# Moving operands of the large matmuls stored as even and odd columns in two halves, in an mLSTM kernel with two gated layers on one core

## The chip, the core and the metric

The kernel runs on one core of a Trainium2 chip. The engines named below are TensorE (matmul; its weight loads are listed apart as PEld), VectorE (DVE), ScalarE (ACT), GpSimd (POOL) and SyncE (SP, which issues most transfers). The metric is the device time of one launch in microseconds; lower is better.

## The reference: what is computed

An mLSTM recurrence over 768 steps for 2 batches and 8 heads of 40 features, and then two gated layers over its 1536 tokens of 320 features:

```python
m_new = np.maximum(f_gate[:, :, t] + m, i_gate[:, :, t])
...
C = f_stab[:, :, None, None] * C + i_stab[:, :, None, None] * np.einsum('bhd,bhe->bhde', vt, kt)
n = f_stab[:, :, None] * n + i_stab[:, :, None] * kt
h_tilde = np.einsum('bhde,bhe->bhd', C, qt)
nq = np.einsum('bhd,bhd->bh', n, qt)[:, :, None]
denom = np.maximum(np.abs(nq), 1.0)
...
y[:, :, t] = o * h_tilde / denom
...
gate = 1.0 / (1.0 + np.exp(-(x @ w_gate)))
val = x @ w_val
return (gate * val @ w_out).astype(np.float32)
...
a = x @ w_a
b = x @ w_b
return (a * b @ w_out).astype(np.float32)
```

## The kernel before

The recurrence is done in 12 chunks of 64 steps (`E`, `S`, `st`, `o` matmuls, small ones). Each chunk gives one token tile of 128 tokens (two batches of 64 steps). A token tile is transposed on TensorE (`transp`, line 482, three 128x128 transposes into PSUM), and the transposed tile is split into a high part, rounded to the chip's fp32r type by ScalarE (`x_hi`, line 486), and a low part, the rest, by VectorE (`x_lo`, line 489). Both go into a block `xb`, which holds `[128 partitions, 2 (high, low), 3 feature chunks, 512 tokens]` of 4 bytes each. Four token tiles fill a block; six blocks serve the two layers.

A unit of a layer takes one 128-wide slice `f` of d_ff and two or four token tiles. `mm1` (line 519) makes the gate (`pa`) and the value (`pb`) in eight matmuls each: the weights are the stationary operand, and a row of `xb` (256 or 512 tokens of one feature chunk) is the moving operand, the one that streams through the array. ScalarE and VectorE make the product `g`, its high part `gh` and its low part `gl`. `mm2` (lines 526 to 528, into `acc`) then multiplies by the output weights: `gh` or `gl` is stationary, and the 320 columns of the output weights (`wh`, the high part, or `wl`, the low part) are the moving operand. Three matmuls go to each token tile, so a unit of four tiles issues 16 matmuls in `mm1` and 12 in `mm2`.

The weights come as 64-bit floats, are narrowed on three engines into 32 bits and split into high and low parts in a tile `W` of 2 x 832 + 256 columns; columns 512 to 831 of each part are the output weights. The host lays the weights out in this order (`pack`) without arithmetic.

The order of all tasks on all engines is written out by hand in `PLAN`. There are 24 units of two token tiles (in `HEAD`, between the chunks of the recurrence) and 60 units of four. In all that is 960 matmuls of 512 columns and 384 of 256 columns in `mm1`, and 864 of 320 columns in `mm2`.

Of the kernel before, what the change touches and what calls it, by code (L numbers as in the profile page):

```python
# [7 lines left out]
F32 = mybir.dt.float32  # L8
BF16 = mybir.dt.bfloat16
F32R = mybir.dt.float32r  # L10
# [3 lines left out]
AF = mybir.ActivationFunctionType  # L14
ALU = mybir.AluOpType

P = 128
# [4 lines left out]
DM = H * D  # L22
DFF = 1536
NF = DFF // P
BT = 512
NB = B * S // BT
NT = BT // P
# [24 lines left out]
NH = 4 * P + DM  # L52
# [78 lines left out]
def kernel(  # L131
# [11 lines left out]
    nc = tc.nc  # L143
# [9 lines left out]
    a3 = ctx.enter_context(tc.tile_pool(name="a3", bufs=3))  # L153
# [7 lines left out]
    def ps_tile(b, name):  # L161
        t = pspool.tile([P, 512], F32, tag=slot(b), name=name)
        fill(t, idle.pop() if idle else 0)
        return t
# [107 lines left out]
    def gate_parts(i):  # L272
        c0, n = GCH[i]
        s0 = 0 if i else 1

        def part0():
            g, lf, L, ms = gws[i]
            if i == 0:
                nc.vector.memset(ms[:, 0:1], -1e30)
                nc.vector.memset(lf[:, 0:1], 0.0)  # L280
            else:
                nc.vector.tensor_copy(ms[:, 0:1], mlast[0])
            nc.vector.tensor_tensor_scan(ms[:, 1:], g[:, 1], g[:, 0], ms[:, 0:1], op0=ALU.add, op1=ALU.max)
            mlast[0] = ms[:, n : n + 1]
            nc.vector.tensor_tensor(lf[:, s0:], g[:, 1, s0:], ms[:, s0:n], op=ALU.add)

        def part1():
            g, lf, L, ms = gws[i]
            nc.vector.tensor_tensor(lf[:, s0:], lf[:, s0:], ms[:, s0 + 1 :], op=ALU.subtract)
            nc.vector.tensor_tensor(g[32:64, 0], g[32:64, 0], ms[32:64, 1:], op=ALU.subtract)  # L290

        def part2():
            g, lf, L, ms = gws[i]
            nc.vector.tensor_tensor_scan(L, rm[:, 0:n], lf, 0.0, op0=ALU.mult, op1=ALU.add)
            nc.vector.tensor_tensor(L[32:64], g[32:64, 0], L[32:64], op=ALU.subtract)

        def part3():
            g, lf, L, ms = gws[i]
            hi = g[:, 1].bitcast(F32R)
            nc.scalar.activation(hi, L, AF.Copy)  # L300
            nc.scalar.activation(lf, hi.bitcast(F32), AF.Copy, scale=cs[0:64, C_AB + 1 : C_AB + 2])

        def part4():
            g, lf, L, ms = gws[i]
            nc.vector.scalar_tensor_tensor(
                V[:, c0 : c0 + n], L, cs[0:64, C_AB : C_AB + 1], lf, op0=ALU.mult, op1=ALU.subtract
            )

        return part0, part1, part2, part3, part4
# [78 lines left out]
    Sps, Eps, Sts, Tps = {}, {}, {}, {}  # L388
# [93 lines left out]
            nc.tensor.transpose(v[:, c], src[:, c * P : (c + 1) * P], ident)  # L482
        return v

    def x_hi(v, dst, c0):
        nc.scalar.activation(dst[:, 0, :, c0 : c0 + P], v, AF.Copy)

    def x_lo(v, dst, c0):
        nc.vector.tensor_tensor(
            dst[:, 1, :, c0 : c0 + P], v, dst[:, 0, :, c0 : c0 + P].bitcast(F32), op=ALU.subtract  # L490
        )

    xb = {}

    def xblock(k):
        if k not in xb:
            xb[k] = a3.tile([P, 2, 3, BT], F32R, tag="xb", name=f"xb{k}")
        return xb[k]

    def ph_T(s):  # L500
        Tps[s] = transp(ps_tile("e", f"tp{s}"), xtok[s])

    def ph_xh(s):
        x_hi(Tps[s], xblock(s // NT), (s % NT) * P)

    def ph_xl(s):
        x_lo(Tps[s], xblock(s // NT), (s % NT) * P)


    def mm1(f, l, m, dst, x):  # L510
        w = W[l * NF + f]
        a, al, c = m * 2 * P, NH + m * 2 * P, 2 * NH + m * P
        seq = (
            (a, 0, 0), (a, 1, 0), (al, 0, 0),
            (a + P, 0, 1), (a + P, 1, 1), (al + P, 0, 1),
            (c, 0, 2), (c, 1, 2),
        )
        for i, (w0, h, cb) in enumerate(seq):
            nc.tensor.matmul(dst, w[:, w0 : w0 + P], x[:, h, cb], start=(i == 0), stop=(i == 7))  # L519

    def mm2(f, l, gh, gl, accs, st, sp):
        w = W[l * NF + f]
        wh, wl = w[:, 4 * P : NH], w[:, NH + 4 * P : 2 * NH]
        for i, a in enumerate(accs):
            c = slice(i * P, (i + 1) * P)
            nc.tensor.matmul(a, gh[:, c], wh, start=st, stop=False)  # L526
            nc.tensor.matmul(a, gh[:, c], wl, start=False, stop=False)  # L527
            nc.tensor.matmul(a, gl[:, c], wh, start=False, stop=sp)  # L528
# [47 lines left out]
    def unit_a(u):  # L576
        k, f = UNITS[u]
        l, st0, ns, fs = SEGS[k]
        x = xblock(l * NB + st0 // NT)[:, :, :, (st0 % NT) * P : (st0 % NT + ns) * P]
        pa = ps_tile("mm1", f"pa{u}")  # L580
        pb = None
        if ns == 2:
            pa, pb = pa[:, 0:256], pa[:, 256:512]
        UT[u] = {"x": x, "pa": pa, "pb": pb}
        mm1(f, l, 0, pa, x)

    def unit_b(u):
        k, f = UNITS[u]
        l, t = SEGS[k][0], UT[u]
        if t["pb"] is None:  # L590
            t["pb"] = ps_tile("e", f"pb{u}")
        mm1(f, l, 1, t["pb"], t["x"])
# [72 lines left out]
    for u, (k, f) in enumerate(UNITS):  # L665
        l, st0, ns, fs = SEGS[k]
# [31 lines left out]
    for i, (c0, n) in enumerate(GCH):  # L698
        if i:
            task(f"gl{i}", "D", lambda i=i: load_gates(i))  # L700
        a, b, c, c2, c3 = gate_parts(i)
# [5 lines left out]
    for i in range(NPREP // 2, NSTEP // 2):  # L707
        s = 2 * i
# [54 lines left out]
    for u, (k, f) in enumerate(UNITS):  # L763
        l, st0, ns, fs = SEGS[k]
        c = l * NF + f
# [20 lines left out]
        for i in range(ns):  # L786
            s = st0 + i
# [25 lines left out]
    with tc.manual_schedule():  # L813
        pick("mm1", ())
        first = ps_tile("mm1", "first")
        for entry in PLAN.split():
            entry, _, n = entry.partition("*")
            name, _, e = entry.partition(":")
# [19 lines left out]
def _layout(inputs):  # L838
    import numpy as np

    f32 = np.float32
    q, k, v, og = (np.asarray(inputs[n]) for n in ("q", "k", "v", "o_gate"))
    ig, fg = np.asarray(inputs["i_gate"]), np.asarray(inputs["f_gate"])
    dt = q.dtype
    a = {}


    r = np.arange(32)
    rpair = np.concatenate([r // 8, r % 16 // 4])
    rb = np.concatenate([r // 4 % 2, r // 2 % 2])  # L850
    rpar = np.concatenate([r % 2, r // 16])
    rlo = np.concatenate([r // 2 % 2, r % 2])

    def rows(g):
        return g[rb, 2 * rpair + rpar]

    a["gates"] = np.stack([rows(ig), rows(fg)], 1)

    def tr(z):

        z = z.reshape(B, NPAIR, 2, NSTEP, T, D).transpose(2, 5, 3, 1, 0, 4)
        o = np.zeros((P, NSTEP, NPAIR * B * T), dt)
        o[:D], o[64 : 64 + D] = z.reshape(2, D, NSTEP, NPAIR * B * T)
        return o.transpose(1, 0, 2)

    a["kqT"] = np.concatenate([tr(k), tr(q)], 2)

    def tok(z):

        z = z.reshape(B, NPAIR, 2, NSTEP, T, D).transpose(2, 4, 3, 1, 0, 5)[::-1]  # L870
        return z.reshape(P, NSTEP, NPAIR * B, D)

    vo = np.ones((P, NSTEP, NPAIR * B, E1 + D), dt)
    vo[..., :D] = tok(v)
    vo[..., E1:] = tok(k)
    a["kv"] = vo.reshape(P, NSTEP, -1).transpose(1, 0, 2)
    a["ogate"] = og.reshape(B, H, NSTEP, T, D).transpose(0, 3, 2, 1, 4).reshape(P, NSTEP * H * D)

    def bits(w):
        w = np.ascontiguousarray(w)  # L880
        return w.view(np.int64) if w.dtype.itemsize == 8 else w

    def pack(x, y, z):
        x, y = (bits(w).reshape(DM, NF, P).transpose(1, 0, 2) for w in (x, y))
        o = np.empty((NF, P, NW), x.dtype)
        for i, w in enumerate((x[:, 0:P], x[:, P : 2 * P], y[:, 0:P], y[:, P : 2 * P])):
            o[:, :, i * P : (i + 1) * P] = w
        o[:, :, 4 * P : NH] = bits(z).reshape(NF, P, DM)
        o[:, 0:64, NH:] = x[:, 2 * P :]
        o[:, 64:, NH:] = y[:, 2 * P :]  # L890
        return o

    a["w1"] = pack(inputs["moe_w_gate"], inputs["moe_w_val"], inputs["moe_w_out"])
    a["w2"] = pack(inputs["moe2_w_a"], inputs["moe2_w_b"], inputs["moe2_w_out"])


    c = np.zeros((P, C_N), f32)
    c[:, C_ID : C_ID + P] = np.eye(P)
    blk = np.zeros((64, NPAIR, B, T), f32)
    blk[np.arange(64), rpair, rb] = 1.0  # L900
    c[0:64, C_RE : C_RE + 512] = blk.reshape(64, 512)
    tri = np.where(np.arange(T)[None, :] < np.arange(T)[:, None], -(2.0**100), 0.0)
    c[64:, C_RE : C_RE + 512] = np.tile(tri, (1, NPAIR * B))
    half = np.arange(P) // 64
    for par in range(2):
        d = c[:, C_LD + par * P : C_LD + (par + 1) * P]
        d[0:32] = (rpar[:32] == par)[:, None]
        tk = half == 1 - par
        d[32:64, tk] = (rpar[32:] == par)[:, None]
        d[64:, tk] = np.eye(64)  # L910
    c[0:D, C_IP : C_AB] = np.eye(D)
    c[64 : 64 + D, C_IP : C_AB] = np.eye(D)
    lo = rlo == 1
    c[0:64, C_AB] = lo
    c[0:64, C_AB + 1] = np.where(lo, 1.0, -1.0)
    a["cst"] = c
    return a
# [21 lines left out]
```

## Time and profile before

| | |
|---|---|
| median of three runs | 475.13 us (473.99 to 476.45) |
| the profiled execution's own time | 474.68 us |
| its span, first to last instruction | 472.9 us |
| TensorE busy | 463.2 us, 98% of the span |
| VectorE, ScalarE, GpSimd busy | 62%, 51%, 21% |
| granted TensorE clock | 0.998 of full speed over the span |

The span leaves out 1.8 us of the execution's own time, which lie around it. [...]

### The profile page before, as it was taken

What the parts mean: (1) busy time and instruction counts of PE and PEld (TensorE: products, weight loads), DVE (VectorE), ACT (ScalarE), POOL (GpSimd) and SP (SyncE); (2) the same over time, 40 slices, a digit from 0 to 9 for tenths busy, and PEclk for the clock granted to TensorE, in tenths of its full rate; (3) what the DMA queues carried; (4) which work ended last, traced back from release to release, by engine and by line L of the source; (5) the groups of instructions that cost most, each with busy time, mean ns of one, the idle gap of its engine ahead of it and who ended that gap; (6) DMA issues with size and microseconds to landing.
All of it is one profiled execution on the core that took longest, in us unless ns stands there. A gap on an engine that the chain in (4) does not pass through costs nothing.

```text
span 472.9 us, 8680 instructions
## 1 busy us (share of the span) xinstructions
PE 463.2 (98%) x3516; PEld 403.6 (85%) x3516; DVE 295.0 (62%) x505; ACT 241.3 (51%) x454; POOL 101.2 (21%) x110
## 2 busy tenths in 40 slices
PE   9899999999999999999999999999999999999995
PEld 3478899999998989888888898888989888888885
DVE  6989997998655663637675564664655727524243
ACT  4899888678672635333464442645453415322130
POOL 3133326623340014100320311103140003200000
PEclk9999999999999999999999999999999999999999
DMA  7979445333022040300202220024021020001121
GB/s 230 308 254 264 150 133 144 88 119 114 1 83 85 1 168 20 130 18 1 83 1 83 75 94 1 9 86 156 10 83 74 1 84 1 0 1 27 30 55 55
DMA packets 10454, 39.31 MB, mean 83 GB/s; under 512 B 1840, under 2 KB 3760, under 8 KB 10416
## 3 DMA queue, kind: packets, MB, share of 16 engines
q1 hardware_dynamic: 10128, 38.45, 25.7%
q8 instruction: 27, 0.44, 0.4%
q10 hardware_dynamic: 288, 0.33, 0.2%
q14 instruction: 11, 0.09, 0.1%
HBM read 36.71 MB, written 1.97 MB: 82 GB/s over the span
## 4 chain that ended last, share of the span: by engine, by line
PE 88%; DVE 4%; DMA 3%; ACT 2%; issue 1%; SPq 0%
PE pa L519 31%; PE pb L519 23%; PE acc L526 9%; PE acc L527 9%; PE acc L528 9%; DMA wst<-in_w_dram 3%; PE o L440 2%; PE sp L411 2%; PE st L430 1%; PE t L482 1%; DVE wst L237 1%; PE e L366 1%; PE tp L482 1%; DVE Z L421 0%; ACT wst L214 0%
## 5 line engine op out<-in xcount | busy, mean ns | idle before, releaser
L519 PE MATMUL pa<-xb,W 128*128 128x512 f32 (+1 forms) x864 | 169.6, 344 | 0.2 <-DVE ge L600 0.2
L519 PEld LDWEIGHTS pa<-xb,W 128*128 128x128 f32 x864 | 136.3, 188 | 19.1 <-DVE ge L600 0.6
L519 PE MATMUL pb<-xb,W 128*128 128x512 f32 x480 | 119.0, 392 | 0.0
L519 PEld LDWEIGHTS pb<-xb,W 128*128 128x128 f32 x480 | 89.0, 188 | 17.9
L555 ACT ACTIVATE gh<-g 128x512 fp32r<-128x512 f32 (+1 forms) x84 | 47.5, 568 | 110.3 <-PE acc L527 55.4
L526 PE MATMUL acc<-W,gh 128*128 128x320 f32 x288 | 89.3, 310 | 0.0
L527 PE MATMUL acc<-W,gh 128*128 128x320 f32 x288 | 88.9, 309 | 0.0
L528 PE MATMUL acc<-W,gl 128*128 128x320 f32 x288 | 88.8, 308 | 0.0
L549 DVE TENSOR_TENSOR g<-g,pb 128x512 f32<-128x512 f32 x60 | 40.9, 685 | 69.8 <-PE pb L519 61.6
L560 DVE TENSOR_TENSOR gl<-g,gh 128x512 fp32r<-128x512 f32 (+1 forms) x66 | 45.5, 694 | 44.0 <-ACT gh L555 43.8
L544 ACT ACTIVATE g<-pa 128x512 f32<-128x512 f32 x60 | 35.6, 595 | 46.1 <-DVE gl L560 38.4
L527 PEld LDWEIGHTS acc<-W,gh 128*128 128x128 f32 x288 | 54.0, 188 | 2.1
L526 PEld LDWEIGHTS acc<-W,gh 128*128 128x128 f32 x288 | 54.0, 188 | 2.0
L528 PEld LDWEIGHTS acc<-W,gl 128*128 128x128 f32 x288 | 54.0, 188 | 0.0
L253 POOL TENSOR_TENSOR W<-wst,W 128x832 fp32r<-128x832 f32 x9 | 19.1, 2124 | 84.5 <-DVE x2tok L634 42.2
L634 DVE SCALAR_TENSOR_TENSOR x2tok<-acc,x2tok 128x320 f32<-128x320 f32 x52 | 23.8, 485 | 19.5 <-PE acc L528 19.5
L237 POOL TENSOR_TENSOR wst<-cva,wst 128x960 int32<-128x960 int32 x7 | 16.9, 2409 | 73.8 <-DVE cva L231 61.1
L213 ACT ACTIVATE cva<-wst 128x960 f32<-128x960 f32 x24 | 25.8, 1075 | 11.2 <-DVE wst L237 10.0
L247 ACT ACTIVATE W<-wst 128x832 fp32r<-128x832 f32 x24 | 23.2, 966 | 11.8 <-DVE wst L237 8.8
L231 DVE SCALAR_TENSOR_TENSOR cva<-wst,cva 128x960 int32<-128x960 int32 x24 | 27.9, 1161 | 0.4
L560 POOL TENSOR_TENSOR gl<-g,gh 128x256 fp32r<-128x256 f32 x18 | 15.4, 860 | 53.5 <-ACT gh L555 48.9
L214 ACT ACTIVATE wst<-wst 128x960 int32<-128x960 uint32 x24 | 26.0, 1085 | 0.0
(85 smaller groups left out, 469.8 us busy)
## 6 DMA issues: line engine op xcount, KB each, us to landing
wst<-in_w_dram SPq DMA_DIRECT2D x24, 960.0 KB
kq<-in_kqT_dram SPq DMA_DIRECT2D x12, 512.0 KB
Y<-in_kv_dram SPq DMA_DIRECT2D x24, 162.0 KB
out_dram<-x2tok SPq DMA_DIRECT2D x10, 160.0 KB
og<-in_ogate_dram SPq DMA_DIRECT2D x1, 960.0 KB
og<-in_ogate_dram SPq DMA_DIRECT2D x1, 640.0 KB
cs<-in_cst_dram SPq DMA_DIRECT2D x1, 469.0 KB
rhsE<-V SPq DMA_DIRECT2D x24, 2.0 KB
```

What stands on the lines that cost most here:

```text
L213: nc.scalar.activation(cva[0], hi.bitcast(F32), AF.Abs)
L214: nc.scalar.activation(lo, lo.bitcast(U32), AF.Copy, scale=2.0**-29)
L231: nc.vector.scalar_tensor_tensor(ai, hi, -0x40000000, ai, op0=ALU.bitwise_and, op1=ALU.bitwise_or)
L519: nc.tensor.matmul(dst, w[:, w0 : w0 + P], x[:, h, cb], start=(i == 0), stop=(i == 7))
L526: nc.tensor.matmul(a, gh[:, c], wh, start=st, stop=False)
L527: nc.tensor.matmul(a, gh[:, c], wl, start=False, stop=False)
L528: nc.tensor.matmul(a, gl[:, c], wh, start=False, stop=sp)
L544: nc.scalar.activation(t, pa, AF.Copy if l else AF.Sigmoid)
L549: nc.vector.tensor_tensor(t, t, pb, op=ALU.mult)
L555: nc.scalar.activation(gh, g, AF.Copy)
L560: eng.tensor_tensor(gl, g, gh.bitcast(F32), op=ALU.subtract)
L634: nc.vector.scalar_tensor_tensor(dst[:, 0:DM], acc, half, dst[:, 0:DM], op0=ALU.mult, op1=ALU.add)
```

## The change

In each `xb` block the tokens of a block are stored with the even tokens in one half of the row and the odd tokens in the other: `[128, 2, 3, 2 (even, odd), 256]`. `x_hi` and `x_lo` read the transposed tile in PSUM at every second column and write 2 x 64 columns where they wrote 128. The host lays the output weights out in the same way, the 160 even columns ahead of the 160 odd ones. The matmuls ask for the columns in their natural order, so a moving operand is read in turn from the first half and from the second: in `mm1` two neighbouring columns lie 256 words (1024 bytes) apart in a partition, in `mm2` 160 words (640 bytes). Stationary operands, outputs in PSUM, the number of instructions and their order on every engine are as before.

```diff
-    def x_hi(v, dst, c0):
-        nc.scalar.activation(dst[:, 0, :, c0 : c0 + P], v, AF.Copy)
-
-    def x_lo(v, dst, c0):
-        nc.vector.tensor_tensor(
-            dst[:, 1, :, c0 : c0 + P], v, dst[:, 0, :, c0 : c0 + P].bitcast(F32), op=ALU.subtract
-        )
+    def halves(v):
+        return v.rearrange("p c (b a) -> p c a b", a=2)
+
+    def x_hi(v, dst, b0):
+        nc.scalar.activation(dst[:, 0, :, :, b0 : b0 + P // 2], halves(v), AF.Copy)
+
+    def x_lo(v, dst, b0):
+        d = dst[:, :, :, :, b0 : b0 + P // 2]
+        nc.vector.tensor_tensor(d[:, 1], halves(v), d[:, 0].bitcast(F32), op=ALU.subtract)
...
-            xb[k] = a3.tile([P, 2, 3, BT], F32R, tag="xb", name=f"xb{k}")
+            xb[k] = a3.tile([P, 2, 3, 2, BT // 2], F32R, tag="xb", name=f"xb{k}")
...
-        x_hi(Tps[s], xblock(s // NT), (s % NT) * P)
+        x_hi(Tps[s], xblock(s // NT), (s % NT) * (P // 2))
...
-        x_lo(Tps[s], xblock(s // NT), (s % NT) * P)
+        x_lo(Tps[s], xblock(s // NT), (s % NT) * (P // 2))
...
-            nc.tensor.matmul(dst, w[:, w0 : w0 + P], x[:, h, cb], start=(i == 0), stop=(i == 7))
+            nc.tensor.matmul(dst, w[:, w0 : w0 + P], x[:, h, cb].rearrange("p a b -> p b a"), start=(i == 0), stop=(i == 7))
...
-        wh, wl = w[:, 4 * P : NH], w[:, NH + 4 * P : 2 * NH]
+        wh, wl = (w[:, k + 4 * P : k + NH].rearrange("p (a b) -> p b a", a=2) for k in (0, NH))
...
-        x = xblock(l * NB + st0 // NT)[:, :, :, (st0 % NT) * P : (st0 % NT + ns) * P]
+        x = xblock(l * NB + st0 // NT)[:, :, :, :, (st0 % NT) * P // 2 : (st0 % NT + ns) * P // 2]
...
-        o[:, :, 4 * P : NH] = bits(z).reshape(NF, P, DM)
+        o[:, :, 4 * P : NH] = bits(z).reshape(NF, P, DM // 2, 2).swapaxes(2, 3).reshape(NF, P, DM)
```

## Rows read from the trace of the kernel before

**Rows 1.** The page, busy time: us, share of the span, instructions.

```profile
span 472.9 us, 8680 instructions
PE 463.2 (98%) x3516; PEld 403.6 (85%) x3516; DVE 295.0 (62%) x505; ACT 241.3 (51%) x454; POOL 101.2 (21%) x110
```

**Rows 2.** The chain that ended last, by line: share of the span.

```profile
PE pa L519 31%; PE pb L519 23%; PE acc L526 9%; PE acc L527 9%; PE acc L528 9%; DMA wst<-in_w_dram 3%; PE o L440 2%; PE sp L411 2%; PE st L430 1%; PE t L482 1%; DVE wst L237 1%; PE e L366 1%; PE tp L482 1%; DVE Z L421 0%; ACT wst L214 0%
```

**Rows 3.** Busy time by stretch; PEclk is the granted clock.

```profile
core 0: us, PE busy (x) PEld busy (x) DVE busy (x) ACT busy (x) POOL busy (x), PEclk, DMA share, GB/s
...
40.00:130.00 90.00, 89.31 (x1228) 84.85 (x1229) 79.23 (x158) 71.89 (x171) 34.91 (x40) 1.00 0.39 119
130.00:467.00 337.00, 337.00 (x1772) 296.51 (x1772) 180.45 (x278) 138.34 (x233) 52.76 (x51) 1.00 0.15 51
```

**Rows 4.** TensorE's waits: total us, times, longest.

```profile
PE first L169 <- DVE zb L173: 1.2, 1, 1.2
PE st L430 <- issue: 1.1, 2, 0.9
...
PE pa L519 <- DVE ge L600: 0.2, 1, 0.2
```

**Rows 5.** Matmuls by shape (moving operand's columns): count, busy us, mean ns.

```profile
L519 PE MATMUL pa<-xb,W 128*128 128x512 f32 x480 | 119.5, 393 | 0.0
L519 PE MATMUL pb<-xb,W 128*128 128x512 f32 x480 | 119.0, 392 | 0.0
L526 PE MATMUL acc<-W,gh 128*128 128x320 f32 x288 | 89.3, 310 | 0.0
L519 PE MATMUL pa<-xb,W 128*128 128x256 f32 x384 | 50.2, 282 | 0.2 <-DVE ge L600 0.2
```

**Rows 6.** The chain in order of time, two stretches: start us, us, what.

```profile
72.31 0.94 PE pa L519 x8
...
348.14 3.66 PE pb L519 x16
```

**Rows 7.** TensorE's timeline, four stretches: start us, us, instruction.

```profile
8.22 3.40 PE L169 MATMUL first<-zb 128*128 128x512 bf16 x15
12.34 0.39 PE L169 MATMUL first<-zb 128*128 128x512 bf16 x1
...
302.03 0.49 PE L482 MATMUL t<-cs,x2tok 128*128 128x128 f32 x3
...
465.75 0.31 PE L527 MATMUL acc<-W,gh 128*128 128x320 f32 x1
...
467.06 0.31 PE L527 MATMUL acc<-W,gh 128*128 128x320 f32 x1
467.21 0.30 PE L528 MATMUL acc<-W,gl 128*128 128x320 f32 x1
```

**Rows 8.** Line 482, the transposes: ns min/median/max, first and last start.

```profile
L482 PE MATMUL t<-cs,x2tok x36: 270/272/273, 237.2 to 306.3; 128*128 128x128 f32 x36
```

**Rows 9.** ScalarE and VectorE by shape: count, busy us, mean ns, idle before.

```profile
L555 ACT ACTIVATE gh<-g 128x512 fp32r<-128x512 f32 x60 | 37.8, 631 | 107.5 <-PE acc L527 55.4 <-DVE g L549 51.9
L555 ACT ACTIVATE gh<-g 128x256 fp32r<-128x256 f32 x24 | 9.8, 411 | 2.8 <-DVE g L551 2.6
L560 DVE TENSOR_TENSOR gl<-g,gh 128x512 fp32r<-128x512 f32 x60 | 42.9, 721 | 43.6 <-ACT gh L555 43.4
L560 DVE TENSOR_TENSOR gl<-g,gh 128x256 fp32r<-128x256 f32 x6 | 2.5, 422 | 0.4 <-ACT gh L555 0.4
L213 ACT ACTIVATE cva<-wst 128x960 f32<-128x960 f32 x24 | 25.8, 1075 | 11.2 <-DVE wst L237 10.0 <-DMA wst<-in_w_dram 1.2
```

**Rows 10.** The tile xb: ns min/median/max, first and last start, forms.

```profile
L486 ACT ACTIVATE xb<-tp x12: 471/486/493, 37.1 to 123.3; 128x384 fp32r<-128x384 f32 x12
L489 DVE TENSOR_TENSOR xb<-tp,xb x12: 501/550/558, 38.5 to 124.2; 128x384 fp32r<-128x384 f32 x12
L486 ACT ACTIVATE xb<-t x12: 486/491/493, 237.7 to 306.6; 128x384 fp32r<-128x384 f32 x12
L489 DVE TENSOR_TENSOR xb<-t,xb x12: 547/557/559, 238.2 to 310.5; 128x384 fp32r<-128x384 f32 x12
```

## The prediction

> **What bounds the kernel now.** The page's busy shares come first: TensorE 98%, VectorE 62%, ScalarE 51%, GpSimd 21% [rows 1]. A busy TensorE need not be the bound, since matmuls overlap, so the chain that ended last is next. Five lines of it, the two of the first product (pa, pb) and the three of the second (acc), make up 81% of the span [rows 2]. The busy time by stretch says where: from 40 us on TensorE has no free time to speak of, at a granted clock of 1.00, while VectorE and ScalarE fall to about half busy behind 130 us [rows 3]. TensorE's waits add up to some 5 us in the whole program, and the one wait of a large matmul is 0.2 us [rows 4]. So from 40 us to the last matmul at 467.2 us [rows 7] the time is what the stream of matmuls takes, and a nanosecond more in each of its matmuls goes to the end of the kernel undiminished.
>
> What the stream takes is read from starts, not durations: a 512-column matmul lasts 392 ns [rows 5], but sixteen of them advance the chain by 3.66 us, 229 ns each [rows 6]. Eight of 256 columns take 0.94 us, 117.5 ns each [rows 6]. Nine of 320 columns lie between 465.75 and 467.06 us, 145.6 ns each [rows 7]. With the counts of the shapes (480 and 480 of 512 columns, 384 of 256, 288 in each of three lines of 320 [rows 5]):
>
> 960 x 0.2288 + 384 x 0.1175 + 864 x 0.1456 = 219.6 + 45.1 + 125.8 = 390.5 us.
>
> That is 390.5 of the 427 us behind 40 us; the rest are the recurrence's small matmuls and the transposes. The columns streamed are 960 x 512 + 384 x 256 + 864 x 320 = 866,304. [...]
>
> **The change part by part.** Instructions, their order and their sizes stay, the transfers too; nothing is moved past a queue and no wait is added. Three things change.
>
> First, x_hi and x_lo read PSUM at every second word and write blocks of 64. They are 24 + 24 instructions of about 0.49 and 0.55 us [rows 10]. ScalarE has a row for reading every second word: the narrowing of 960 elements of a wide tile takes 1075 ns [rows 9]. Contiguous instructions of the same kind, 631 ns for 512 and 411 ns for 256 [rows 9], give 0.859 ns an element and would make it 411 + 704 x 0.859 = 1016 ns. The stride costs 59 ns, 6%. Lower bound of this part: nothing. Upper bound: each of the 48 instructions takes twice its streaming part, 24 x 384 x (0.859 + 1.168) = 19 us, of which TensorE would see only what it waits for; it waits for the chain behind these tiles 0.2 us in all [rows 4]. I take 0 on the path. If that cover were gone, the first four tiles, ahead of the first unit at 40 us, would add up to 3 us.
>
> Second, the moving operands of mm1: two neighbouring columns now lie 1024 bytes apart. Third, those of mm2, 640 bytes apart. No row shows TensorE reading like that; all its moving operands here are contiguous. [...] For the upper side there are the rates at which engines of this trace take in 4-byte words one at a time. TensorE itself, in the transposes of full f32 words: three 128-column transposes take 0.49 us [rows 7] and one lasts 0.272 us [rows 8], so they start 0.109 us apart, 0.85 ns a column. ScalarE: 0.859 ns an element, as above. VectorE: (721 - 422) / 256 = 1.168 ns [rows 9].
>
> The prices, on 866,304 columns: at 0.434 ns a column (the slope between the 256- and the 512-column matmuls, (228.8 - 117.5) / 256) nothing is added. If a column that comes from another place than the one before takes two cycles, 0.833 ns, each column adds 0.417 ns: 866,304 x 0.417 = 361 us. With the slope of 0.434 it is 377 us. At VectorE's 1.168 ns it is 866,304 x 0.734 = 636 us. I take two cycles, because the transposes and ScalarE both stand at 0.85 ns, twice TensorE's column, and those are the rows that are nearest to an operand taken word by word. The stationary operands don't change, and their loads (188 ns long, overlapped) would only have more time.
>
> [...] The ScalarE row says that a stride by itself is all but free: 6%, by which the kernel would stay at 475 us if TensorE behaved alike. [...] No run so far shows which holds for TensorE.
>
> Sum for the likeliest: 474.7 us, the profiled execution's own time, + 361 + 0 = 836 us. The median of the three runs is 0.4 us higher, which changes nothing.
>
> **The rivals.**
>
> *No penalty.* [...] For it: the stride on ScalarE costs 6% [rows 9], the pattern has only two places in turn, and the weights' loads leave the engine's own reading undisturbed. [...] Time: 475 us, up to 3 more through x_hi and x_lo.
>
> *Only a part pays.* The two distances, 1024 and 640 bytes, may not collide alike. If mm1 alone paid the second cycle: 589,824 columns x 0.417 = 246 us, 720 us in all. If mm2 alone: 276,480 x 0.417 = 115 us, 590 us. A penalty of half a cycle on all comes to 655 us.
>
> *Dearer than two cycles.* If each word cost what a word costs on VectorE, the time would be 475 + 636 = 1111 us. Against it: nothing in TensorE's rows takes so long for a column. For it: TensorE's column is the shortest step of all readers here, so a fixed time for each separate fetch costs it the most columns. [...]
>
> *Faster.* The same 512 columns of 2-byte data start (3.40 - 0.39) / 14 = 215 ns apart [rows 7] where the 4-byte ones take 229. If those 14 ns are a collision of successive reads in one place, reading two places in turn would remove it: 0.027 ns on each of 866,304 columns, 23 us, hence 451 us. It decides only if the alternate reads cost less than those 0.027 ns. [...]
>
> **How the numbers follow.** A measurement of this kernel tells about 0.5%, 2.4 us, from no change. Two cycles a column: 0.47. No penalty: 0.17. Only a part or less than a cycle: 0.13. Dearer: 0.20. Faster: 0.03. The predicted time is the first, 836 us. Its own range is 805 (the 13 ns at each matmul's end hidden behind the longer stream, 29 us) to 875 (the steeper slope, and 20 us of x_hi and x_lo that show). The range for 8 in 10 leaves out the faster case and nearly all of the dearer one: 473 to 900 us, which holds 0.47 + 0.17 + 0.13 and the cheapest tenth of the dearer, 0.79. Faster by over 0.5%: 0.03. Within 0.5%: 0.15, nearly all of the case without penalty, the rest of which x_hi and x_lo push past 2.4 us. Slower: 0.82.
>
> **What the profile after would show.** If it is two cycles: eight 512-column matmuls advance the chain by some 3.5 us instead of 1.83, 320-column ones start some 280 ns apart and 256-column ones 225; small matmuls, transposes and weight loads keep their times; VectorE and ScalarE wait longer for TensorE and their busy shares fall to some 35% and 29%; the granted clock stays at 1.00. If x_hi and x_lo matter, their mean rises above 0.49 and 0.55 us and TensorE shows a wait that ends with xb. The prediction is wrong if the starts keep their distances (no penalty), if 320 and 512 columns differ in their price per column (a part pays), or if the price per column is far from 0.83 ns. [...]

## The result and the profile after

The changed kernel takes 457.6 us (456.9 to 457.9 in four runs) against 474.6 us before: a ratio of 0.963, 95% interval 0.9605 to 0.966. It is faster by 17 us, where I had forecast a slower kernel at 836 us.

The profiled execution's own time is 457.4 us. The page of the changed kernel, its span, busy shares and the chain that ended last by line (lines 519 and 526 to 528 are now 523 and 530 to 532):

```profile
span 455.6 us, 8675 instructions
PE 440.4 (97%) x3511; PEld 393.1 (86%) x3516; DVE 304.4 (67%) x505; ACT 257.1 (56%) x454; POOL 102.9 (23%) x110
PE pa L523 24%; PE pb L523 19%; PE acc L532 7%; PE acc L530 7%; PE acc L531 7%; DMA wst<-in_w_dram 3%; DVE wst L237 2%; DVE g L555 1%; DVE cva L231 1%; ACT cva L213 1%; ACT W L247 1%; ACT wst L214 1%; ACT Dt L373 1%; DVE gl L564 1%; PE sp L411 1%
```

TensorE is still the bound, but the five lines of the large matmuls make up 64% of the chain instead of 81% [rows 2], and lines of VectorE and ScalarE have come into it. VectorE and ScalarE are busy for longer than before, 304 and 257 us instead of 295 and 241 [rows 1], with the same instructions.

The chain in order of time, where it runs through large matmuls (start us, us, what):

```profile
126.62 3.57 PE pa L523 x32
...
200.08 3.45 PE pb L523 x16
```

TensorE's timeline near the end (start us, us, instruction):

```profile
448.09 0.30 PE L530 MATMUL acc<-W,gh 128*128 128x320 f32 x1
...
449.31 0.30 PE L530 MATMUL acc<-W,gh 128*128 128x320 f32 x1
```

The 512-column matmuls now take 3.45 / 16 = 216 ns each of the chain, where they took 229; those of 256 columns 3.57 / 32 = 112 ns instead of 117.5 [rows 6]; nine of 320 columns 1.22 us, 136 ns each, instead of 146 [rows 7]. At 216 ns the 4-byte columns take what 2-byte ones took before, 215 [rows 7]. The stream now takes 960 x 0.2156 + 384 x 0.1116 + 864 x 0.1356 = 367.0 us, 23.5 us less than the 390.5 before. The span shrank by 17.3 us. So some 6 us were given back.

TensorE's idle time shows them: it rose from 9.7 us (472.9 - 463.2 [rows 1]) to 15.2 us (455.6 - 440.4). By stretch, in the columns of [rows 3]:

```profile
40.00:130.00 90.00, 87.03 (x1238) 81.60 (x1235) 80.73 (x156) 72.35 (x168) 35.74 (x40) 1.00 0.38 119
130.00:449.00 319.00, 316.90 (x1772) 289.28 (x1771) 187.85 (x277) 153.72 (x235) 53.99 (x51) 1.00 0.16 54
```

Between 40 and 130 us TensorE is idle for 3.0 us instead of 0.7, and behind 130 us for 2.1 us instead of none. The longest of the waits behind 130 us, 1.1 us, ends at 319.50 us. Its row among TensorE's waits, in the columns of [rows 4], and the chain leading to it (start us, us, what):

```profile
PE pa L523 <- ACT g L548: 1.4, 2, 1.1
...
305.39 1.31 ACT W L247
...
310.14 1.47 DVE cva L231
...
316.31 1.49 ACT cva L213
...
318.97 0.49 ACT g L548
...
319.50 1.99 PE pa L523 x8
```

TensorE waits here for ScalarE's `g`, and ScalarE is late: narrowing a weight tile takes it longer (that this is the cause is shown further down, by the version without the give-back). The row of line 247 before, among groups by shape, and behind it the rows of lines 213 (1075 ns before [rows 9]) and 247 in the changed kernel:

```profile
L247 ACT ACTIVATE W<-wst 128x832 fp32r<-128x832 f32 x24 | 23.2, 966 | 11.8 <-DVE wst L237 8.8 <-POOL wst L237 3.0
...
L213 ACT ACTIVATE cva<-wst 128x960 f32<-128x960 f32 x24 | 31.2, 1299 | 13.9 <-DVE wst L237 10.8 <-DMA wst<-in_w_dram 2.4 <-POOL wst L237 0.6
...
L247 ACT ACTIVATE W<-wst 128x832 fp32r<-128x832 f32 x24 | 28.6, 1193 | 14.6 <-DVE wst L237 10.9 <-POOL wst L237 3.6
```

The change doesn't touch these instructions. What they have in common is that they read every second 4-byte word of the wide weight tile. VectorE's line 231, which reads it in the same way, went from 1161 to 1258 ns.

### The profile page after: what moved, and what is told of

Same layout as the page of the kernel before. It is cut to its first block, busy times and chain, and to the rows that moved or that the text cites. A ratio compares the mean times of both kernels' runs of the same rounds, so it can differ in the third digit from the quotient of the medians.

```text
span 455.6 us, 8675 instructions
## 1 busy us (share of the span) xinstructions
PE 440.4 (97%) x3511; PEld 393.1 (86%) x3516; DVE 304.4 (67%) x505; ACT 257.1 (56%) x454; POOL 102.9 (23%) x110
## 4 chain that ended last, share of the span: by engine, by line
PE 68%; DVE 13%; ACT 11%; DMA 3%; issue 2%; POOL 1%; SPq 0%; DVEq 0%; POOLq 0%; ACTq 0%
PE pa L523 24%; PE pb L523 19%; PE acc L532 7%; PE acc L530 7%; PE acc L531 7%; DMA wst<-in_w_dram 3%; DVE wst L237 2%; DVE g L555 1%; DVE cva L231 1%; ACT cva L213 1%; ACT W L247 1%; ACT wst L214 1%; ACT Dt L373 1%; DVE gl L564 1%; PE sp L411 1%
## 5 line engine op out<-in xcount | busy, mean ns | idle before, releaser
L523 PE MATMUL pa<-xb,W 128*128 128x512 f32 (+1 forms) x864 | 161.2, 335 | 2.2 <-ACT g L548 1.4
L523 PEld LDWEIGHTS pa<-xb,W 128*128 128x128 f32 x864 | 134.5, 190 | 15.7 <-ACT g L548 2.2
L523 PE MATMUL pb<-xb,W 128*128 128x512 f32 x480 | 112.6, 380 | 0.6 <-DVE g L553 0.6
L532 PE MATMUL acc<-W,gl 128*128 128x320 f32 x288 | 86.7, 301 | 0.3 <-POOL gl L564 0.2
L530 PE MATMUL acc<-W,gh 128*128 128x320 f32 x288 | 86.7, 301 | 0.0
L531 PE MATMUL acc<-W,gh 128*128 128x320 f32 x288 | 86.1, 299 | 0.0
L564 DVE TENSOR_TENSOR gl<-g,gh 128x512 fp32r<-128x512 f32 (+1 forms) x66 | 48.2, 737 | 42.1 <-ACT gh L559 41.9
L213 ACT ACTIVATE cva<-wst 128x960 f32<-128x960 f32 x24 | 31.2, 1299 | 13.9 <-DVE wst L237 10.8
L247 ACT ACTIVATE W<-wst 128x832 fp32r<-128x832 f32 x24 | 28.6, 1193 | 14.6 <-DVE wst L237 10.9
L214 ACT ACTIVATE wst<-wst 128x960 int32<-128x960 uint32 x24 | 31.5, 1312 | 0.0
L231 DVE SCALAR_TENSOR_TENSOR cva<-wst,cva 128x960 int32<-128x960 int32 x24 | 30.2, 1258 | 0.4
```

Source lines behind the costliest of these rows:

```text
L213: nc.scalar.activation(cva[0], hi.bitcast(F32), AF.Abs)
L214: nc.scalar.activation(lo, lo.bitcast(U32), AF.Copy, scale=2.0**-29)
L231: nc.vector.scalar_tensor_tensor(ai, hi, -0x40000000, ai, op0=ALU.bitwise_and, op1=ALU.bitwise_or)
L247: nc.scalar.activation(w[:, 0:NH], g[:, 0:NH], AF.Copy)
L523: nc.tensor.matmul(dst, w[:, w0 : w0 + P], x[:, h, cb].rearrange("p a b -> p b a"), start=(i == 0), stop=(i == 7))
L564: eng.tensor_tensor(gl, g, gh.bitcast(F32), op=ALU.subtract)
```

## The experiments

Three questions were open: what makes the matmuls faster, why the stride costs nothing, and what slows ScalarE.

**One operand at a time.** The first kernel keeps only `xb` in halves, the second only the output weights.

```diff
 e1_mm1_only: the change, without
-        wh, wl = (w[:, k + 4 * P : k + NH].rearrange("p (a b) -> p b a", a=2) for k in (0, NH))
...
-        o[:, :, 4 * P : NH] = bits(z).reshape(NF, P, DM // 2, 2).swapaxes(2, 3).reshape(NF, P, DM)
 e2_mm2_only: the kernel before, with these two lines alone
```

In the first, the two lines of the kernel before stand in their place.

> Only the first product's operand (xb) is kept in two halves; the output weights are contiguous as before. Theory A (a moving operand of 4-byte words collides with itself when it is read in sequence, 0.02 to 0.03 ns a column, and reading two places in turn removes it): 512-column matmuls start 216 ns apart, 256-column ones 112, 320-column ones stay at 146; that takes 960 x 13 + 384 x 6 = 14.8 us off the stream, some of it given back in waits, so 460 to 465 us. Rival B (only the distance of the output weights, 640 bytes, matters, or the gain comes from elsewhere): 475 us.

> Only the output weights are kept in two halves; xb is contiguous as before. Theory A: 320-column matmuls start 136 ns apart instead of 146, the others stay at 229 and 118; 864 x 10 = 8.6 us off the stream, so 466 to 469 us, and the two runs' gains add up to more than the whole change's 17 us if waits gave some of it back. Rival B: the whole gain comes from the first product, so 475 us here.

With `xb` alone: 464.7 us, ratio 0.977 (0.973 to 0.981). With the output weights alone: 466.8 us, 0.982 (0.977 to 0.987). Each keeps its own part of the gain. The two gains, 10.9 and 8.8 us against the 475.6 of the kernel before beside them, add up to 19.7, more than the whole change's 17, but with some 2 us of uncertainty on each that surplus isn't clear of the noise. In the first the 320-column matmuls stay at 147 ns and the 512-column ones go to 216; in the second it is the other way round: they last 300 ns instead of 310 there, and 392 as before. ScalarE's line 213 takes 1288 ns in the first (groups by shape), 1082 in the second: the slowing belongs to `xb` alone.

```profile
L213 ACT ACTIVATE cva<-wst 128x960 f32<-128x960 f32 x24 | 30.9, 1288 | 12.6 <-DVE wst L237 10.2 <-DMA wst<-in_w_dram 1.9 <-POOL wst L237 0.5
```

**Read patterns by themselves.** A kernel of TensorE alone, all other engines idle behind the start, streams 48 matmuls of each pattern; the operand `M` holds words of the kernel's inputs, and the starts of two neighbouring patterns, divided by 48, give one matmul.

```python
c = M[:, 0:512]
...
run("flat", c.rearrange("p (b a) -> p b a", a=2))      # contiguous
run("half", c.rearrange("p (a b) -> p b a", a=2))      # two halves in turn
...
run("four", c.rearrange("p (a b) -> p b a", a=4))      # four quarters in turn
...
run("jtwo", c.rearrange("p (a b j) -> p b a j", a=2, j=2))   # two words of each half in turn
...
run("stwo", M[:, 0:1024].rearrange("p (b s) -> p b s", s=2)[:, :, 0])   # every second word
```

> Leaves out the whole computation: TensorE alone streams 48 matmuls of each of some thirty read patterns, one after another, with the other engines idle; the time means nothing, the distance of the starts does. Theory A (the moving operand's own words collide): 512 contiguous 4-byte columns start 229 ns apart and in two halves 216, whatever the distance of the halves, with nothing else running; 2-byte columns 216 either way. Theory B (the moving operand's reads collide with the loads of the stationary operand): with 64 or 32 stationary columns the contiguous case falls towards 216, and a stationary operand read with a stride changes it. Theory C (other engines' or the transfers' reads and writes collide with it): the contiguous case is at 216 here, as nothing else runs. [...]

TensorE's timeline of that kernel (start us, us, instruction, number):

```profile
29.44 10.52 PE L165 MATMUL bcont<-Mb,Wb 128*128 128x512 bf16 x47
39.80 23.41 PE L165 MATMUL bhalf<-Mb,Wb 128*128 128x512 bf16 x48
62.59 11.52 PE L165 MATMUL cont<-M,Wt 128*128 128x512 f32 x48
73.95 11.04 PE L165 MATMUL flat<-M,Wt 128*128 128x512 f32 x48
84.83 10.52 PE L165 MATMUL half<-M,Wt 128*128 128x512 f32 x48
95.19 10.52 PE L165 MATMUL far<-M,Wt 128*128 128x512 f32 x48
105.55 13.75 PE L165 MATMUL four<-M,Wt 128*128 128x512 f32 x48
119.13 10.53 PE L165 MATMUL lfour<-M,Wt 128*128 128x512 f32 x48
...
181.29 16.47 PE L165 MATMUL jtwo<-M,Wt 128*128 128x512 f32 x48
197.59 12.18 PE L165 MATMUL jfour<-M,Wt 128*128 128x512 f32 x48
...
232.80 21.91 PE L165 MATMUL stwo<-M,Wt 128*128 128x512 f32 x48
254.54 22.32 PE L165 MATMUL sfour<-M,Wt 128*128 128x512 f32 x48
...
333.41 11.20 PE L165 MATMUL wsixty<-M,Wt 128*64 128x512 f32 x48
344.45 11.29 PE L165 MATMUL wthirty<-M,Wt 128*32 128x512 f32 x48
355.58 11.96 PE L165 MATMUL wturn<-M,Wt 128*128 128x512 f32 x48
367.37 11.76 PE L165 MATMUL wturnhalf<-M,Wt 128*128 128x512 f32 x48
```

Contiguous (flat): (84.83 - 73.95) / 48 = 227 ns. The contiguous run ahead of it (cont) comes to 237 by this sum, but its start at 62.59 us seems to be recorded some 0.46 us early: the next one follows 0.69 us later, and after a few they lie 227 ns apart. In halves: 216, at 1024 bytes as at 8192 (far) and at 16 (lfour). So the 11 ns between the two are there with nothing else running: theory C, other engines and transfers, falls. With 64 or 32 stationary columns instead of 128 (wsixty, wthirty) the contiguous operand takes 230 and 232 ns: theory B, the weights' loads, falls as the cause of the 11 ns here (13 in the kernel). Its other sign did come: a stationary operand read with a step of 8 words makes the contiguous case 246 (wturn) and the halves 242 (wturnhalf), so loads read that way do hold the stream up. But the doubling that I had priced does exist: every second word (stwo) takes 453 ns, every fourth (sfour) 461, twice the contiguous time. Four places in turn take 283, two words of each half in turn (jtwo) 340, and 2-byte columns in halves (bhalf) 484 against 216 (by its own starts), where theory A had 216 for both. Of the 4-byte patterns only single words from two places in turn reach 216 ns.

**Columns in pairs.** These times would fit if what counts were the step from a column to the next but one: one word in two halves (216 ns), two in a contiguous operand (227), four where every second word is read (453). Two far places read with a step of 2 words in each would then take 227 ns, and with a step of 4 some 450. The next kernel tries it: two places 8192 bytes apart, each read with a step of 1, 2, 3, 4 and 6 words.

```python
q = M.rearrange("p (a n) -> p n a", a=2)
...
for st, nm in ((2, "ptwo"), (3, "pthree"), (4, "pfour"), (6, "psix")):
    run(nm, q[:, 0 : 256 * st].rearrange("p (n s) a -> p n s a", s=st)[:, :, 0])
```

> Leaves out the whole computation: more read patterns alone on TensorE, then four reads of every second word by ScalarE and by VectorE beside eight patterns. [...] Eight places in turn: 283 or more, as four. Theory Q (it is the change of place that helps, whatever the step): steps 2, 3, 4 and 6 in two far places stay near 216. [...]

TensorE's timeline of that kernel:

```profile
51.40 10.52 PE L165 MATMUL pone<-M,Wt 128*128 128x512 f32 x48
61.76 11.08 PE L165 MATMUL ptwo<-M,Wt 128*128 128x512 f32 x48
72.67 16.48 PE L165 MATMUL pthree<-M,Wt 128*128 128x512 f32 x48
88.98 21.83 PE L165 MATMUL pfour<-M,Wt 128*128 128x512 f32 x48
110.62 21.78 PE L165 MATMUL psix<-M,Wt 128*128 128x512 f32 x48
132.22 22.27 PE L165 MATMUL pairstep<-M,Wt 128*128 128x512 f32 x48
154.30 26.75 PE L165 MATMUL eight<-M,Wt 128*128 128x512 f32 x48
180.85 21.85 PE L165 MATMUL stwoten<-M,Wt 128*128 128x512 f32 x48
```

Step 1: 216 ns; step 2: 227, as the contiguous operand; step 3: 340; step 4: 451; step 6: 450; neighbouring pairs 8 words apart (pairstep): 460. Steps 2 and 4 take what the step between every second column let expect, and theory Q (216 throughout) falls at step 2. How the engine fetches these columns, the times don't show.

An estimate from the step of 4 ties the times together: 451 / 4 = 113 ns for each word of the step. It gives 338 ns at step 3 and 226 at step 2, where 340 and 227 were measured. At step 1 it would be 113, less than the 216 measured there, and at step 6 676, more than the 450 measured there: the time follows the step from 2 to 4 words, and at 1 and 6 it doesn't. By this estimate the time of a contiguous operand is set by its step of two words, and the halves take that limit away, down to the 216 ns that 2-byte columns take too (bcont). For 320 and 256 contiguous columns the same sum gives 141 and 113 ns where the kernel before has 146 and 118, so it is not the whole account.

What the step doesn't give is the time where every second column itself goes to and fro. In four quarters in turn it alternates between two places 256 words apart; at the price of the large steps that would be 450 ns, and it takes 283. Two words of each half in turn take 340, eight places in turn 553, more than any step. That stays open.

**Who is held up.** First ScalarE and VectorE read 960 words beside an idle TensorE, a contiguous operand and one in halves.

```python
wide = raw[:, 1024:2944]
...
copy(d[:, 0], wide.rearrange("p (n x) -> p n x", x=2)[:, :, 1])   # "sec", five times
...
copy(e2, wide[:, 0:960])                                          # "lin", five times
```

> Leaves out the whole computation: ScalarE and then VectorE run five reads of every second word (960) and five of 960 contiguous words, while TensorE is idle, streams a contiguous operand, and streams one in two halves. Theory A2 (TensorE reading in two halves takes turns of the memory from an engine that reads every second word): ScalarE's strided read lasts about as long with TensorE idle as with a contiguous operand (1.07 us) and some 20% longer with the halves, the contiguous read stays. Rival (the slower ScalarE rows of the changed kernel come from the timing of transfers or of VectorE and GpSimd): no difference between the three.

Groups of that kernel by shape (count, busy us, mean ns, idle before):

```profile
L190 ACT ACTIVATE secacthalf<-raw 128x960 f32<-128x960 f32 x5 | 7.4, 1477 | 0.1
L192 DVE TENSOR_TENSOR secdvehalf<-raw,z 128x960 f32<-128x960 f32 x5 | 7.2, 1437 | 0.1
...
L192 DVE TENSOR_TENSOR secdvecont<-raw,z 128x960 f32<-128x960 f32 x5 | 5.8, 1156 | 0.1
...
L190 ACT ACTIVATE secactcont<-raw 128x960 f32<-128x960 f32 x5 | 5.4, 1080 | 0.1
L190 ACT ACTIVATE secactidle<-raw 128x960 f32<-128x960 f32 x5 | 5.3, 1061 | 0.1
...
L190 ACT ACTIVATE linacthalf<-raw 128x960 f32<-128x960 f32 x5 | 5.0, 1002 | 0.1
```

ScalarE's strided read goes from 1080 to 1477 ns beside the halves, VectorE's from 1156 to 1437; contiguous reads stay at 1.0 and 1.16 us. The times are those that theory A2 named, with a larger price than I gave (37% and 24%). TensorE's granted clock was 0.902 on average over that kernel: the single 512-column matmuls at 42.38 and 56.02 us, in a stretch in which TensorE was nearly idle, last 0.80 us, those from 74.12 us on 0.39 or 0.40, and the 1080 ns reads began right behind the one at 56.02; in the kernel of the steps, at 1.00, the same read beside a contiguous operand takes 1063 ns. That kernel then repeated the strided reads beside eight operands (groups by shape):

```profile
L214 ACT ACTIVATE secacttwofiftysix<-raw 128x960 f32<-128x960 f32 x4 | 5.9, 1478 | 0.1
L214 ACT ACTIVATE secacteightkib<-raw 128x960 f32<-128x960 f32 x4 | 5.9, 1478 | 0.1
L214 ACT ACTIVATE secactkib<-raw 128x960 f32<-128x960 f32 x4 | 5.9, 1478 | 0.1
...
L214 ACT ACTIVATE secactwout<-raw 128x960 f32<-128x960 f32 x4 | 4.4, 1104 | 0.1
L214 ACT ACTIVATE secactsixtyfour<-raw 128x960 f32<-128x960 f32 x4 | 4.3, 1082 | 0.1
L214 ACT ACTIVATE secactbf<-raw 128x960 f32<-128x960 f32 x4 | 4.3, 1080 | 0.1
L214 ACT ACTIVATE secactsixteen<-raw 128x960 f32<-128x960 f32 x4 | 4.3, 1066 | 0.1
```

All of the operands in halves stream at 216 ns for 512 columns, or 136 for 320. But with the two places 256, 1024 or 8192 bytes apart the neighbour is held up, and with 16, 64 or 640 it is not, or by 4% at most. VectorE's rows there say the same: 1436 ns at the first three, 1155 or 1156 at the others. TensorE's shorter time by itself is not the reason, since a 2-byte operand at 216 ns (secactbf) leaves ScalarE at 1080. 640 is the distance of the output weights, with which the second kernel above left ScalarE alone (1082 ns).

**A version without the give-back.** Two kernels move only the distance of the halves of `xb`, to 64 bytes and to 1152.

```diff
 e6_near: runs of 16 words in turn
-        return v.rearrange("p c (b a) -> p c a b", a=2)
+        return v.rearrange("p c (g b a) -> p c g a b", a=2, b=16)
...
-            xb[k] = a3.tile([P, 2, 3, 2, BT // 2], F32R, tag="xb", name=f"xb{k}")
+            xb[k] = a3.tile([P, 2, 3, BT // 32, 2, 16], F32R, tag="xb", name=f"xb{k}")
...
 e9_padded: 32 words of padding
-            xb[k] = a3.tile([P, 2, 3, 2, BT // 2], F32R, tag="xb", name=f"xb{k}")
+            xb[k] = a3.tile([P, 2, 3, 2, BT // 2 + 32], F32R, tag="xb", name=f"xb{k}")
```

> The whole change, but the even and odd tokens of a block lie in turn in runs of 16 words, so that two neighbouring columns of the first product are read 64 bytes apart instead of 1024; the output weights as in the change. Theory D (ScalarE's and VectorE's reads of every second word are held up only when TensorE's two places lie a whole multiple of 256 bytes apart): the three ScalarE rows of the narrowing return from 1.19 to 1.31 us to 0.97 to 1.09 us, the matmuls keep 216, 112 and 136 ns, the waits given back shrink and the time is 451 to 454 us. Rival (the shorter stream itself starves TensorE of its inputs, whatever ScalarE reads): 457 us, as the change.

> The change with 32 unused words between the two halves of xb, so that the places lie 1152 bytes apart, four and a half times 256. If the distance modulo 256 bytes decides (theory D): as the run with 64 bytes, 451 to 454 us with ScalarE's rows at their old length. If the shortness of the distance decides: 457 us, ScalarE's rows as long as in the change.

> The changed kernel itself, beside the two above on the same chip: 457 us, 0.963 of the kernel before.

At 64 bytes: 452.2 us, ratio 0.951 (0.949 to 0.954). Padded to 1152 bytes: 452.2 us, 0.952 (0.949 to 0.955). The change itself beside them: 458.4 us, 0.963 (0.9605 to 0.966). The two intervals lie clear below the third. ScalarE's row in the first of them (groups by shape; 1107 ns in the second):

```profile
L213 ACT ACTIVATE cva<-wst 128x960 f32<-128x960 f32 x24 | 26.3, 1097 | 11.2 <-DVE wst L237 9.6 <-DMA wst<-in_w_dram 1.3 <-POOL wst L237 0.3
```

The span of its profiled execution is 448.8 us, 24.1 less than before, and the medians of the two runs lie 22.8 and 22.7 us below the 474.9 beside them: the 23.5 us of the stream arrive nearly whole. The rival, that a shorter stream starves TensorE of itself, falls, and so does the short distance as the reason: 1152 bytes do as well as 64.

**Four places in the kernel.** The output weights alone, in four quarters; the edit is against the kernel before.

```diff
-        wh, wl = w[:, 4 * P : NH], w[:, NH + 4 * P : 2 * NH]
+        wh, wl = (w[:, k + 4 * P : k + NH].rearrange("p (a b) -> p b a", a=4) for k in (0, NH))
...
-        o[:, :, 4 * P : NH] = bits(z).reshape(NF, P, DM)
+        o[:, :, 4 * P : NH] = bits(z).reshape(NF, P, DM // 4, 4).swapaxes(2, 3).reshape(NF, P, DM)
```

> The kernel before with only the output weights stored anew, in four quarters read in turn instead of two halves. [...] If reading in turn from several places helps as such: 466 us, as with two halves.

It takes 496.1 us, ratio 1.044 (1.039 to 1.048). TensorE's timeline near its end:

```profile
485.20 0.34 PE L526 MATMUL acc<-W,gh 128*128 128x320 f32 x1
...
486.74 0.34 PE L526 MATMUL acc<-W,gh 128*128 128x320 f32 x1
```

Nine matmuls in 1.54 us are 171 ns each, 25 more than before; 864 x 0.0255 = 22 us of the 21 that were lost. An estimate from the 283 ns of four quarters, 283 / 512 x 320 = 177 ns, is 6 too many. That reading from several places helps as such (466 us) falls. For the step between every second column the run is no further test.

## Why the prediction was wrong

**What bounds the kernel** was right: the starts of the large matmuls set the time, and each nanosecond of them went to the end until other engines came in the way.

**The step that failed** is "If a column that comes from another place than the one before takes two cycles". It put 0.417 ns more on each column; measured were 0.026 ns less, (229 - 216) / 512. I took two successive columns as two successive reads of one reader. By the runs of the steps, what counts is every second column: the change turns a step of two words into a step of one, and the time of a 512-column matmul from 229 to 216 ns. The doubling that I priced exists, 453 ns for every second word, but the change is a pattern that avoids it. A layout with a step of four words between every second column would take some 850 us, near my 836 (an estimate from its 451 ns, not run). No run shows the two cycles of 0.833 ns and the 0.417 ns more that the sum is made of, nor the 13 ns at each matmul's end in its range; the runs showed 0.42 ns a column in all in halves (216 / 512) and 0.45 before (229 / 512).

**The rows for the bounds** were badly chosen. The transposes' 0.85 ns a column and ScalarE's 0.859 ns an element are times of other operations, and twice what the changed operand takes: 216 / 512 = 0.42 ns a column. The row that bore on it was the one I used for the faster rival, 215 ns for 2-byte columns against 229 [rows 7], and I gave it too little weight. What the change took off, 6, 10 and 13 ns at 256, 320 and 512 columns, grows with the columns, as a price per column does.

**The faster rival**, at 3 in 100, is what happened: the stream became 23.5 us shorter, where I had worked out 23. The size came from the right row; the mechanism was told as a collision of successive reads in one place, which the steps of 1 and 2 words put right: two places help at a step of one word (216 ns) and not at two (227). Its 451 us missed the 457.6 by what was given back.

**x_hi and x_lo** cost nothing, as I took it: 24 instructions each at 0.49 and 0.55 us, as in [rows 10]. Of the two signs that I had named for them one did appear, a wait of TensorE that ends with `xb` (1.2 us), but it is gone in the run at 64 bytes, whose x_hi and x_lo take as long. What I had not costed at all is the neighbour: narrowing, with a stride that the change doesn't touch, became 21% dearer on ScalarE and 8% on VectorE's line 231, and that cost 6 us.

**What the profile would show**: VectorE and ScalarE did not fall to 35% and 29% but rose to 67% and 56%; the clock stayed at 1.00, as named. It did so too in the kernel of patterns, where every second and every fourth word took 453 and 461 ns: its granted clock was 1.00.

## What to carry to other kernels

Compare the time of a matmul for 2-byte and 4-byte operands and for several column counts: 215 against 229 ns showed the gain of this change, which was 6, 10 and 13 ns at 256, 320 and 512 columns. Here a 4-byte (fp32r) moving operand was fastest where every second column was contiguous (216 ns against 227); reading in turn from two places does that, from four it took 283. Try distances of the two places other than those that held the neighbours up here (256, 1024 and 8192 bytes), and look at the neighbours' strided reads: here 64 or 1152 instead of 1024 bytes was worth another 6 us.

## What the runs showed of the hardware

A 4-byte (fp32r) moving operand of 512 columns takes 216, 227, 340 and 451 ns for a step of 1, 2, 3 and 4 words between every second column. A contiguous operand that starts one word later in its tile takes 237 ns instead of 227 (in halves: 217 and 216). A stationary operand read with a step of 8 words (wturn, above) makes it 246. ScalarE's and VectorE's reads of every second word last 37% and 24% longer beside an operand whose two places lie 256, 1024 or 8192 bytes apart, and by 4% at most at 16, 64 and 640 bytes; in the kernel 1152 bytes gave ScalarE's rows back too (1107 ns instead of 1299). All of this fits a distance of whole multiples of 256 bytes, but the three that hold others up are also powers of two, and a distance such as 768 bytes was not run. Why such a distance matters, no run here shows.
